# Retention and a two-layer MLP in split fp32: first products of two token blocks side by side in one 512-column matmul, in the second half of the weight units

## The chip, the cores and the metric

The kernel runs on one core of a Trainium2 chip. The metric is the device time of one execution in microseconds, the median of several. TensorE (PE in the profile) multiplies: a stationary operand of 128x128 is loaded (PEld), a moving operand of up to 512 columns streams against it, and the result goes to one of eight PSUM banks of 512 fp32 columns. ScalarE (ACT), VectorE (DVE) and GpSimd (POOL) do the elementwise work; SyncE (SP) issues nearly all DMAs.

## The reference

The first part is retention without softmax over 8 batches, 8 heads, 576 positions and 64 dimensions; its output, as 4608 tokens of 512, goes through a two-layer MLP of width 2048 with a PReLU whose slope depends on the channel.

```python
scores = scale * np.matmul(q, k.transpose(0, 1, 3, 2))
Dmat = np.where(rel >= 0, gamma[:, None, None] ** rel[None, :, :], 0.0)
x = np.matmul(scores * Dmat, v)                    # -> (4608, 512)
h = x @ w_in                                       # 512 -> 2048
g = np.maximum(h, 0.0) + alpha * np.minimum(h, 0.0)
out = g @ w_out                                    # 2048 -> 512
```

## The kernel before, in words

**Split products.** To keep fp32 precision at the faster rate of the fp32r type, each fp32 operand of the MLP is split into pieces (`split_x`, `split_g`, `split_w`), three planes that TensorE reads as fp32r. A product is then three matmuls in place of one: two go into one PSUM bank or half bank, the third into another, and an elementwise step joins the two.

**Tiling.** Tokens are cut into 18 blocks of 256 (`kb`). The hidden width is cut into eight *units* of 256 (`u`), each with four weight tiles: two for the first product, two for the second. Weights in three planes don't all fit, so the work is done in *visits*: visits 0 to 16 take blocks 0 to 16 with units 0 to 3 and keep the partial output in DRAM (`o_kept`); visit 17 takes block 17 with all eight units; visits 18 to 34 take blocks 0 to 16 again with units 4 to 7 and add the partial output (`evacuate`). A visit with one unit is a *cell*. The first eight cells are done in plain fp32 (`unit_plain`, L991, and `second_plain`, L1022), while weights are still converted.

**A cell.** `unit` makes the first product: for each half `f` of the unit, 12 matmuls of 256 columns (three planes, four parts of the 512 inputs) into bank `psh[f]`, whose two halves take the two sums (L1056). Then four operations on 256 columns: ScalarE copies one sum (L1063), VectorE joins (L1064), ScalarE takes the Relu of the negative into PSUM (L1067), VectorE applies the slope (L1070). `split_g` makes the three planes of g: two ScalarE multiplies (L1079, L1081) and two GpSimd subtractions (L1083, L1086). `second` makes the second product, 12 matmuls of 512 columns into the four banks `pso` (L1107), which gather over the units of a visit; the last cell of a visit is followed by `evacuate` (L1125, L1130) and a store. The second product of a cell comes `LAG` = 2 cells after its first.

**x.** `fetch_x` loads a block's x (or takes it from the retention stage), `split_x` makes its planes in one of two buffers `lxs`: ScalarE L957 and L961 or L969, VectorE L964, GpSimd L971 and L974. From visit `LATE_X` on the banks `psa` serve as scratch.

**Retention.** The first eight pairs of heads are done in a start-up phase (`part_...`, L447 to L595); the others one by one between the cells (`joint`, L808, L859 to L869), at the cells listed in `todo`. They use banks `psa` and `psh`.

**Order.** The text emits operations with estimated costs (`do`); `plan` then runs a list schedule over all of them: it works out due times from the end backwards and gives every engine its fixed order of instructions. TensorE may be taken up to `AHEAD_PE` operations ahead of the text. Engines run their own order and wait for each other by semaphores; `lock=True` marks operations of GpSimd and VectorE that are ordered against each other.

Of the kernel before, what the change touches and what calls it, by code (L numbers as in the profile page):

```python
# [16 lines left out]
ACTF = mybir.ActivationFunctionType  # L17
# [4 lines left out]
def kernel(  # L22
# [58 lines left out]
    def piece(x):  # L81
        return x.bitcast(PIECE)
# [108 lines left out]
    def do(eng, cost, fn, r=(), w=(), late=0.0, lock=False, kind=None, hold=0.0):  # L191
        deps, gens = set(), []
        for keys, writes in ((r, False), (w, True)):
            for g, *sub in keys:
                wr, rd = g.keys.setdefault(tuple(sub), ([], []))
                deps.update(wr)
                if writes:
                    deps.update(rd)
                deps.update(g.before)
                if g not in gens:  # L200
                    gens.append(g)
        op = Op(eng, cost, fn, None, [g.slot for g in gens if g.slot and g.slot.bank], late, lock, hold)
        for g, *sub in w:
            g.keys[tuple(sub)] = ([op], [])
        for g, *sub in r:
            g.keys[tuple(sub)][1].append(op)
        for g in gens:
            assert not g.slot or g.slot.gen is g
            g.ops.append(op)
        op.deps = [d for d in deps if d is not op]  # L210
        op.gens, op.kind = gens, kind or eng
        ops.append(op)
        return op
# [123 lines left out]
    AHEAD_PE = 150  # L337
    BACKLOG, HOLD = 2.0, 30.0
    LAG, HOLD_X = 2, 100.0
    GROUPS = (("v0",), ("v1",), ("x", "su"))  # L340
    SLACK, SWITCH = {"PE": 0.3}, {"PE": 0.1}
    BEGIN = {"PE": 5.0, "ACT": 0.5, "DVE": 8.2, "POOL": 5.8, "SP": 0.5}
# [395 lines left out]
    def w_piece(u, i, l):  # L738
        g, n = w_at[u, i][l]
        return piece(words_of(g)[:, n * DM:(n + 1) * DM])  # L740
# [207 lines left out]
                [(xkm[kb], 0)], [(x, 0)])  # L948
        vis["from"] = x

    def split_x(vis):
        x = vis["from"]
        to = vis["x"] = Gen(lxs[vis["n"] % 2])
        keys = [(x, *s) for s in x.keys]
        for n in range(2):
            c = slice(2 * n, 2 * n + 2)
            do("ACT", 0.64, lambda c=c: nc.scalar.mul(piece(to.get()[:, 0, c]), x.get()[:, c],  # L957
                                                      BELOW * 2.0 ** -12), keys, [(to, 0, n)])
            if vis["n"] >= LATE_X:
                h = Gen(psa[n])  # L960
                do("ACT", 0.6, lambda c=c, h=h: nc.scalar.mul(  # L961
                    piece(h.get()), x.get()[:, c].rearrange("p c t -> p (c t)"), BELOW), keys,
                    [(h, 0)])
                do("DVE", 0.7, lambda c=c, h=h: nc.vector.tensor_tensor(  # L964
                    out=piece(to.get()[:, 1, c].rearrange("p c t -> p (c t)")),
                    in0=x.get()[:, c].rearrange("p c t -> p (c t)"), in1=h.get(),
                    op=ALU.subtract), keys + [(h, 0)], [(to, 1, n)])
            else:
                do("ACT", 0.64, lambda c=c: nc.scalar.mul(piece(to.get()[:, 2, c]), x.get()[:, c],  # L969
                                                          BELOW), keys, [(to, 2, n)])  # L970
                do("POOL", 1.29, lambda c=c: nc.gpsimd.tensor_tensor(  # L971
                    out=piece(to.get()[:, 1, c]), in0=x.get()[:, c], in1=to.get()[:, 2, c],
                    op=ALU.subtract), keys + [(to, 2, n)], [(to, 1, n)], lock=True)
            do("POOL", 1.29, lambda c=c: nc.gpsimd.tensor_tensor(  # L974
                out=piece(to.get()[:, 2, c]), in0=to.get()[:, 0, c], in1=to.get()[:, 1, c],
                op=ALU.subtract), [(to, 0, n), (to, 1, n)], [(to, 2, n)], lock=True)


    def unit_plain(cell):
# [60 lines left out]

    def unit(cell):
        vis, u = cell["vis"], cell["u"]
        x = vis["x"]
        ga = Gen(gas[cell["n"] % 2])
        for f in range(2):
            ph = Gen(psh[f])

            def at(b, ph=ph):
                return ph.get()[:, b * TB:(b + 1) * TB]

            def mm(f=f, at=at):
                for n, (b, l) in enumerate(((0, 0), (1, 2), (0, 1))):
                    for cc in range(NCC):
                        w = w_piece(u, cc // 2, l)
                        c0 = (cc % 2 * 2 + f) * P
                        nc.tensor.matmul(at(b), w[:, c0:c0 + P],  # L1056
                                         piece(x.get()[:, l, cc]), start=(n == 0 and cc == 0),
                                         stop=(n > 0 and cc == NCC - 1), skip_group_check=True)
            do("PE", 1.43, mm, [(x, l, n) for l in range(3) for n in range(2)] +
               [w_at[u, i][l] for i in range(2) for l in range(3)], [(ph, 0), (ph, 1)], kind="pieces")  # L1060
            fc = 2 * u + f
            g = lambda f=f: ga.get()[:, f]
            do("ACT", 0.36, lambda g=g, at=at: nc.scalar.copy(g(), at(1)), [(ph, 1)], [(ga, f)])  # L1063
            do("DVE", 0.42, lambda g=g, at=at: nc.vector.scalar_tensor_tensor(  # L1064
                out=g(), in0=at(0), scalar=ONE, in1=g(), op0=ALU.mult, op1=ALU.subtract),
                [(ph, 0)], [(ga, f)])
            do("ACT", 0.39, lambda g=g, at=at: nc.scalar.activation(at(1), g(), ACTF.Relu,  # L1067
                                                                    scale=-1.0),
               [(ga, f)], [(ph, 1)])
            do("DVE", 0.48, lambda g=g, at=at, fc=fc: nc.vector.scalar_tensor_tensor(  # L1070
                out=g(), in0=at(1), scalar=malpha[:, fc:fc + 1], in1=g(), op0=ALU.mult,
                op1=ALU.add), [(ph, 1), (cst, "a")], [(ga, f)])
        cell["ga"] = ga

    def split_g(cell):
        ga = cell["ga"]
        to = cell["g"] = Gen(gs[cell["n"] % 3])
        both = [(ga, 0), (ga, 1)]
        do("ACT", 0.64, lambda: nc.scalar.mul(piece(to.get()[:, 2]), ga.get(), BELOW), both,  # L1079
           [(to, 2)])  # L1080
        do("ACT", 0.64, lambda: nc.scalar.mul(piece(to.get()[:, 0]), ga.get(), BELOW * 2.0 ** -12),  # L1081
           both, [(to, 0)])
        do("POOL", 1.29, lambda: nc.gpsimd.tensor_tensor(  # L1083
            out=piece(to.get()[:, 1]), in0=ga.get(), in1=to.get()[:, 2], op=ALU.subtract),
            both + [(to, 2)], [(to, 1)], lock=True)
        do("POOL", 1.29, lambda: nc.gpsimd.tensor_tensor(  # L1086
            out=piece(to.get()[:, 2]), in0=to.get()[:, 0], in1=to.get()[:, 1], op=ALU.subtract),
            [(to, 0), (to, 1)], [(to, 2)], lock=True)
# [168 lines left out]

    ready_kb = [((kb + 1) * TB - 1) // S for kb in range(NKB)]
    todo = {}
    for i, at in enumerate((8, 10, 12, 14, 16, 18, 20, 22, 25, 27, 29, 31, 33, 35, 37, 39, 41, 43, 45, 47, 49, 51, 53, 55)):  # L1260
        todo.setdefault(at, []).append(2 * NPAIR + 1 + i)
    assert sum(map(len, todo.values())) == len(pairs) - 2 * NPAIR

# [21 lines left out]
    def planes():  # L1285
        for x in (kxs, qxs, kns[0], kns[1], kTs[0], kTs[1], qTs[0], qTs[1]):
            yield Gen(x), 0
        for x in (ats, xs[4]):
            g = Gen(x)
            yield g, 0  # L1290
            yield g, 1

    def start_x(vis):
        kb = vis["kb"]
        if "from" not in vis and (kb not in xb or NPAIR * (ready_kb[kb] + 1) in done):
            fetch_x(vis)

    pend = []
    for cell in cells[8:]:
        n, vis = cell["n"], cell["vis"]  # L1300
        start_x(vis)
        if "x" not in vis:
            split_x(vis)
        for _ in range(ahead.get(n, 0)):
            convert((op_, 0), was, None)
        for at in late.get(n, ()):
            if at == 16:
                plane = planes()
            split_w(at, raw_room(), [next(plane) for _ in range(3)] if at < 20 else None)
        unit(cell)  # L1310
        pend.append(cell)
        if len(pend) > LAG:
            second(pend.pop(0))
        split_g(cell)
        for x in todo.get(n, ()):
            joint_(x)
        nxt = vis["n"] + 1
        if nxt < len(visits) and (cell["last"] or vis["n"] > 3):
            start_x(visits[nxt])
            if "from" in visits[nxt] and "x" not in visits[nxt] and cell["last"]:  # L1320
                split_x(visits[nxt])
    for cell in pend:
        second(cell)
    best = plan()

    port = None
# [39 lines left out]
```

## Time and profile before

| | |
|---|---|
| median of 3 runs | 949.26 us (947.74 to 952.68) |
| the profiled execution | 948.37 us, of which its span is 946.7 us |
| TensorE busy, granted clock | 924.4 us (98%), 1.00 |
| VectorE, ScalarE, GpSimd busy | 549.3, 572.0, 576.6 us |
| first products, 256 columns (L1056) | 2832 matmuls in the largest group, 284 ns each |
| second products, 512 columns (L1107) | 1416 matmuls in the largest group, 392 ns each |
| DMA | 121.06 MB, 128 GB/s |

The durations of matmuls overlap their neighbours, so that their sum says nothing of the pace; the distance between the starts of two does. Busy shares are averages over stages: the first 108 us are start-up, then retention and MLP alternate up to about 442 us, the rest is MLP alone.

### The profile page before, as it was taken

The page shows a single profiled execution, that of the slowest core. Times are in us where ns is not written, and L with a number is a line of the kernel's source. Part 1 is how long each engine was busy: PE and PEld are TensorE (multiplying, and loading weights), DVE is VectorE, ACT ScalarE, POOL GpSimd, SP SyncE. Part 2 cuts the span into 40 slices and gives each one's busy share as a digit, 9 for nine tenths or more (in the row PEclk, how much of TensorE's full clock was granted, in tenths as well). Part 3 has the DMA queues.
Part 4 walks back from the last instruction along what each step waited for, and adds up shares of the span by engine and source line. Part 5 has one row for each costly group of instructions (what it writes and reads, how often), then busy time and mean ns, then how long its engine had stood idle before and what let it go on. Part 6 is the DMA issues. An engine that isn't in the chain of part 4 may idle for free.

```text
span 946.7 us, 22947 instructions
## 1 busy us (share of the span) xinstructions
PE 924.4 (98%) x9009; PEld 817.5 (86%) x9009; DVE 549.3 (58%) x1180; ACT 572.0 (60%) x1285; POOL 576.6 (61%) x473
## 2 busy tenths in 40 slices
PE   5899999999999999999999999999999999999998
PEld 4566688988898899888999999999999999999997
DVE  6667566666677676677655844444445444444444
ACT  4465556557666566667867875555555555555443
POOL 3757766738767666746764475555555555555543
PEclk9999999999999999999999999999999999999999
DMA  9967587876878878874433511222222222122211
GB/s 225 226 182 132 142 186 164 183 166 164 204 177 183 199 166 200 192 179 147 145 123 123 179 36 50 83 86 83 67 68 68 68 67 68 68 67 68 67 46 68
DMA packets 235533, 121.06 MB, mean 128 GB/s; under 512 B 203408, under 2 KB 203424, under 8 KB 235424
## 3 DMA queue, kind: packets, MB, share of 16 engines
q1 hardware_dynamic: 233312, 119.05, 48.4%
q8 instruction: 71, 1.16, 0.5%
q10 hardware_dynamic: 2112, 0.53, 0.3%
q14 instruction: 38, 0.31, 0.1%
HBM read 74.19 MB, written 31.98 MB: 112 GB/s over the span
## 4 chain that ended last, share of the span: by engine, by line
PE 92%; DMA 3%; ACT 2%; SPq 1%; DVE 1%; issue 0%; POOL 0%; ACTq 0%; DVEq 0%
PE psh L1056 41%; PE pso L1107 39%; PE psh L808 3%; PE pso L1022 3%; PE psh L991 2%; PE psa L869 2%; SPq L220 1%; ACT x L571 1%; DMA w<-in_q_dram 1%; PE psh L859 1%; PE psa L866 1%; DMA lx<-in_moe_w_out_dram 0%; DMA w<-in_k_dram 0%; DMA lx<-in_moe_w_in_dram 0%; DMA w<-in_moe_w_in_dram 0%
## 5 line engine op out<-in xcount | busy, mean ns | idle before, releaser
L1056 PEld LDWEIGHTS psh<-lx,w 128*128 128x128 f32 x2832 | 355.9, 191 | 11.4 <-issue 0.5
L1056 PE MATMUL psh<-lx,w 128*128 128x256 f32 x2832 | 363.7, 284 | 0.1
L1107 PE MATMUL pso<-w,g 128*128 128x512 f32 x1416 | 347.8, 392 | 0.0
L1083 POOL TENSOR_TENSOR g<-ga,g 128x512 fp32r<-128x512 f32 x136 | 175.7, 1292 | 240.6 <-ACT g L1079 212.7
L1107 PEld LDWEIGHTS pso<-w,g 128*128 128x128 f32 x1416 | 257.1, 189 | 47.9
L1064 DVE SCALAR_TENSOR_TENSOR ga<-psh,ga 128x256 f32<-128x256 f32 x272 | 114.8, 422 | 212.6 <-ACT ga L1063 209.6
L1063 ACT COPY ga<-psh 128x256 f32<-128x256 f32 x272 | 101.4, 373 | 160.3 <-PE psh L1056 145.2
L1086 POOL TENSOR_TENSOR g<-g 128x512 fp32r<-128x512 f32 x136 | 176.0, 1294 | 16.2 <-DVE wa L690 2.8
L1070 DVE SCALAR_TENSOR_TENSOR ga<-psh,malpha,ga 128x256 f32<-128x256 f32 x272 | 130.3, 479 | 57.5 <-ACT psh L1067 55.8
L1067 ACT ACTIVATE psh<-ga 128x256 f32<-128x256 f32 x272 | 105.8, 389 | 71.0 <-DVE ga L1064 70.5
L1079 ACT ACTIVATE g<-ga 128x512 fp32r<-128x512 f32 x136 | 85.9, 632 | 55.2 <-DVE ga L1070 46.8
L974 POOL TENSOR_TENSOR lx<-lx 128x512 fp32r<-128x512 f32 x66 | 85.3, 1295 | 38.4 <-DVE lx L964 30.6
L1081 ACT ACTIVATE g<-ga 128x512 fp32r<-128x512 f32 x136 | 84.3, 620 | 0.0
L887 DVE SCALAR_TENSOR_TENSOR at<-psa,pf,mask 64x512 f32<-64x512 f32 x48 | 36.0, 750 | 21.4 <-PE psa L866 20.2
L957 ACT ACTIVATE lx<-x 128x512 fp32r<-128x512 f32 x66 | 41.1, 628 | 0.0
L808 PEld LDWEIGHTS psh<-at,vn 128*64 128x64 f32 x864 | 27.5, 138 | 8.9 <-issue 6.4
L780 POOL TENSOR_TENSOR qx<-qx,tabx 128x576 f32<-128x576 f32 x24 | 27.5, 1147 | 12.1 <-DVE wa L690 7.6
L971 POOL TENSOR_TENSOR lx<-x,lx 128x512 fp32r<-128x512 f32 x24 | 31.0, 1293 | 6.2 <-ACT lx L969 5.2
L808 PE MATMUL psh<-at,vn 128*64 128x64 f32 x864 | 31.4, 225 | 0.5 <-DVE ga L1070 0.5
L964 DVE TENSOR_TENSOR lx<-x,psa 128x512 fp32r<-128x512 f32 x42 | 28.4, 677 | 3.3 <-PE psh L1056 2.1
L1056 PE MATMUL psh<-lx,kT 128*128 128x256 f32 x144 | 29.0, 283 | 0.0
L869 PE MATMUL psa<-vn,kn 64*64 64x64 f32 x768 | 28.5, 223 | 0.0
(210 smaller groups left out, 1085.9 us busy)
## 6 DMA issues: line engine op xcount, KB each, us to landing
xk<-x SPq DMA_DIRECT2D x18, 512.0 KB, 4.3
out_dram<-o SPq DMA_DIRECT2D x36, 256.0 KB, 2.0
ok<-o SPq DMA_DIRECT2D x34, 256.0 KB, 3.4
x<-xk SPq DMA_DIRECT2D x17, 512.0 KB, 5.0
op<-ok SPq DMA_DIRECT2D x17, 512.0 KB, 3.9
qx<-in_q_dram SPq DMA_DIRECT2D x96, 72.0 KB, 2.9
kx<-in_k_dram SPq DMA_DIRECT2D x96, 72.0 KB, 2.7
kn<-in_k_dram SPq DMA_DIRECT2D x48, 144.0 KB, 3.3
```

The lines of the kernel that those rows point to most:

```text
L808: nc.tensor.matmul(pv[i].get()[half(h2), (j - js[0]) * C:(j - js[0] + 1) * C], vns[n % 2][:, h2, j], mt.get()[:, h2, j], start=True, stop= ...
L974: do("POOL", 1.29, lambda c=c: nc.gpsimd.tensor_tensor(out=piece(to.get()[:, 2, c]), in0=to.get()[:, 0, c], in1=to.get()[:, 1, c], op=ALU. ...
L1056: nc.tensor.matmul(at(b), w[:, c0:c0 + P], piece(x.get()[:, l, cc]), start=(n == 0 and cc == 0), stop=(n > 0 and cc == NCC - 1), skip_grou ...
L1063: do("ACT", 0.36, lambda g=g, at=at: nc.scalar.copy(g(), at(1)), [(ph, 1)], [(ga, f)])
L1064: do("DVE", 0.42, lambda g=g, at=at: nc.vector.scalar_tensor_tensor(out=g(), in0=at(0), scalar=ONE, in1=g(), op0=ALU.mult, op1=ALU.subtrac ...
L1067: do("ACT", 0.39, lambda g=g, at=at: nc.scalar.activation(at(1), g(), ACTF.Relu, scale=-1.0), [(ga, f)], [(ph, 1)])
L1070: do("DVE", 0.48, lambda g=g, at=at, fc=fc: nc.vector.scalar_tensor_tensor(out=g(), in0=at(1), scalar=malpha[:, fc:fc + 1], in1=g(), op0=A ...
L1079: do("ACT", 0.64, lambda: nc.scalar.mul(piece(to.get()[:, 2]), ga.get(), BELOW), both, [(to, 2)])
L1081: do("ACT", 0.64, lambda: nc.scalar.mul(piece(to.get()[:, 0]), ga.get(), BELOW * 2.0 ** -12), both, [(to, 0)])
L1083: do("POOL", 1.29, lambda: nc.gpsimd.tensor_tensor(out=piece(to.get()[:, 1]), in0=ga.get(), in1=to.get()[:, 2], op=ALU.subtract), both + [ ...
L1086: do("POOL", 1.29, lambda: nc.gpsimd.tensor_tensor(out=piece(to.get()[:, 2]), in0=to.get()[:, 0], in1=to.get()[:, 1], op=ALU.subtract), [( ...
L1107: nc.tensor.matmul(a[2 * m + b].get(), piece(g.get()[:, l, f, m * P:(m + 1) * P]), w_piece(u, 2 + f, l), start=(cell["first"] and f == 0 a ...
```

## The change

After visit 17, visits are taken in pairs: 18 with 19, up to 32 with 33; visit 34 is left alone. For a pair the planes of x of both blocks are laid side by side (`two_rooms`): in the two `lxs` buffers for odd pairs, in the four weight slots of unit 3, which is no longer needed, for even ones. A first product (`unit_two`) then takes 512 columns, both blocks at once, into two whole banks: `psh` for the first half of a unit, `psa` for the second. The four elementwise operations work on 512 columns. Their result goes to one of five rooms (`ga_room`: three x buffers and the two buffers of v that retention has left), since a cell of the second block waits until the first block's four cells are done. The second products stay as they are for each cell, but are drawn from a queue (`pump`), so many after each half unit as `PUMP` says; `split_g` is done for the two cells at the queue's head. `split_x` makes its pieces in SBUF alone, with a VectorE subtraction, where it fills such a pair. Some planes of late weights move to other buffers (`planes`), and the cells at which the pairs of heads begin are respaced (`todo`).

The diff, cut to its core:

```diff
+    PUMP0, PUMP = ((1, 1), (0, 1), (0, 1), (0, 1)), ((1, 2), (1, 2), (0, 1), (0, 1))
...
+    def two_rooms(n):
+        if n % 2:
+            gg = [Gen(x) for x in lxs]
+            return {(l, cc): (gg[cc // 2], (l * 2 + cc % 2) * DM)
+                    for l in range(3) for cc in range(NCC)}, DM
+        gg = [Gen(wsl[NS - 1, i]) for i in range(4)]
+        at = {(2, cc): (gg[cc], 2 * DM) for cc in range(NCC)}
+        at.update({(l, cc): (gg[l * 2 + cc // 2], cc % 2 * DM)
+                   for l in range(2) for cc in range(NCC)})
+        return at, DM
...
+                    eng, cost, tt = (("POOL", 1.29, nc.gpsimd) if rooms is None else
+                                     ("DVE", 0.69 if wide else 0.42, nc.vector))
+                    do(eng, cost, lambda c=c, l=l, d=d, tt=tt: tt.tensor_tensor(
+                        out=piece(l()), in0=raw(c), in1=d(), op=ALU.subtract),
+                        keys + key(2, c), key(1, c), lock=True)
...
+    def unit_two(va, vb, u, ga, f):
+        at_x = va["x"][0]
+        p0, p1 = (Gen(x) for x in (psa if f else psh))
+
+        def mm():
+            for p, l in ((p0, 0), (p1, 2), (p0, 1)):
+                for cc in range(NCC):
+                    w = w_piece(u, cc // 2, l)
+                    c0 = (cc % 2 * 2 + f) * P
+                    g, o = at_x[l, cc]
+                    nc.tensor.matmul(p.get(), w[:, c0:c0 + P], piece(words_of(g)[:, o:o + DM]),
+                                     start=(l != 1 and cc == 0), stop=(l > 0 and cc == NCC - 1))
+        do("PE", 2.755, mm, x_keys(va, 0) + x_keys(vb, 1) +
+           [w_at[u, i][l] for i in range(2) for l in range(3)], [(p0, 0), (p1, 0)], kind="pieces")
+        fc = 2 * u + f
+        g = lambda: words_of(ga)[:, f * DM:(f + 1) * DM]
+        do("ACT", 0.59, lambda: nc.scalar.copy(g(), p1.get()), [(p1, 0)], [(ga, f)])
+        do("DVE", 0.69, lambda: nc.vector.scalar_tensor_tensor(
+            out=g(), in0=p0.get(), scalar=ONE, in1=g(), op0=ALU.mult, op1=ALU.subtract),
+            [(p0, 0)], [(ga, f)])
+        do("ACT", 0.62, lambda: nc.scalar.activation(p1.get(), g(), ACTF.Relu, scale=-1.0),
+           [(ga, f)], [(p1, 0)])
+        do("DVE", 0.75, lambda: nc.vector.scalar_tensor_tensor(
+            out=g(), in0=p1.get(), scalar=malpha[:, fc:fc + 1], in1=g(), op0=ALU.mult,
+            op1=ALU.add), [(p1, 0), (cst, "a")], [(ga, f)])
...
-        to = cell["g"] = Gen(gs[cell["n"] % 3])
+        to = cell["g"] = Gen(gs[ng[0] % 3])
+        ng[0] += 1
...
-    for i, at in enumerate((8, 10, 12, 14, 16, 18, 20, 22, 25, 27, 29, 31, 33, 35, 37, 39, 41, 43, 45, 47, 49, 51, 53, 55)):
+    for i, at in enumerate((8, 10, 12, 14, 16, 18, 20, 22, 24, 26, 29, 31, 33, 35, 37, 39, 42, 44, 46, 48, 50, 52, 54, 56)):
...
+    queue = list(pend)
+
+    def ahead_g(k=2):
+        for c in queue[:k]:
+            if "ga" in c and "g" not in c:
+                split_g(c)
+
+    def pump(k):
+        for _ in range(k):
+            if queue and "ga" in queue[0]:
+                ahead_g(1)
+                second(queue.pop(0))
+                ahead_g()
+
+    for i, (va, vb) in enumerate(two):
+        ca, cb = of[va["n"]], of[vb["n"]]
+        queue += ca + cb
+        for nu, (a, b) in enumerate(zip(ca, cb)):
+            ga = ga_room()
+            for f in range(2):
+                unit_two(va, vb, a["u"], ga, f)
...
+                    ahead_g()
+                pump((PUMP if i else PUMP0)[nu][f])
+            nxt = va["n"] + 2 + (nu - 1)
+            if nu in (1, 2) and nxt < len(visits):
+                next_x(visits[nxt])
```

## The prediction

> **What bounds the kernel now.** I read the page first: engine shares, the forty slices, the chain, the costliest groups.
>
> ```profile
> PE 924.4 (98%) x9009; PEld 817.5 (86%) x9009; DVE 549.3 (58%) x1180; ACT 572.0 (60%) x1285; POOL 576.6 (61%) x473
> ...
> PE   5899999999999999999999999999999999999998
> PEld 4566688988898899888999999999999999999997
> ...
> PEclk9999999999999999999999999999999999999999
> ...
> PE 92%; DMA 3%; ACT 2%; SPq 1%; DVE 1%; issue 0%; POOL 0%; ACTq 0%; DVEq 0%
> ```
>
> TensorE is busy in every slice but the first two, at full granted clock, and carries 92% of the chain that ended last. No other engine passes 61%. A change therefore pays only if it shortens TensorE's own work, and costs only if it makes TensorE wait. The list of TensorE's waits shows that nearly all of them lie in the start-up:
>
> ```profile
> PE psa L447 <- DMA w<-in_k_dram: 4.3, 1, 4.3
> PE psh L991 <- ACT x L571: 3.3, 2, 2.0
> PE pso L447 <- POOL w L423: 3.3, 2, 2.9
> ...
> PE psh L808 <- DVE ga L1070: 0.5, 1, 0.5
> ```
>
> L447 and L991 are start-up code; L808 is the only entry of the stage after it. The stretch that is changed begins near 450 us. Its table of windows and its timeline of TensorE:
>
> ```profile
> 600.00:900.00 300.00, 300.00 (x1928) 274.00 (x1928) 140.68 (x291) 167.89 (x372) 173.41 (x136) 1.00 0.21 69
> ```
>
> ```profile
> 700.88 3.04 PE L1056 MATMUL psh<-lx,w 128*128 128x256 f32 x24
> 703.75 0.63 PE L1107 MATMUL pso<-qT,g 128*128 128x512 f32 x2
> ...
> 706.50 3.04 PE L1056 MATMUL psh<-lx,w 128*128 128x256 f32 x24
> 709.37 2.91 PE L1107 MATMUL pso<-w,g 128*128 128x512 f32 x12
> ```
>
> The columns of the first are TensorE, weight load, VectorE, ScalarE, GpSimd: TensorE is never idle in 300 us, VectorE is busy 47%, ScalarE 56%, GpSimd 58%. In the second the start times give the true pitch, because durations overlap: 24 first-product matmuls of 256 columns take 703.75 - 700.88 = 2.87 us (119.6 ns each), 12 second-product matmuls of 512 columns 706.50 - 703.75 = 2.75 us (229.2 ns each). A cell costs 5.62 us and nothing waits.
>
> **The change, part by part.**
>
> *First products side by side.* The visits 18 to 33 make eight pairs; each has four weight units and two halves of a unit, so 64 calls of `unit_two` with 12 matmuls of 512 columns. They replace 128 half units of 12 matmuls of 256 columns, 1536 instructions by 768. The shape (128x128 weights, 512 moving columns, the same piece type) is that of the second product, so I take its 2.75 us for twelve. Two cells then cost 2 x 2.75 = 5.50 us in place of 2 x 2.87 = 5.74 us: 0.24 us for each of 32 pairs of cells, **7.7 us** (0.01 us of reading error on each start makes this 7 to 8.5).
>
> A rule speaks against that. The Trainium skill, "TensorE: Matmul & The Clock Gate", section "Back-to-back issue gap", gives the gap of an isolated matmul as its columns over 2.4 GHz and about 2.5 ns more. Joining two matmuls would then save 2.5 ns, and 768 joins 1.9 us: too little to see. The rows above have 2 x 119.6 - 229.2 = 10 ns. The rows are of this stream, with its own weight loads, so I keep 10 ns; the rule gives the low end of the gain.
>
> *Evacuating them.* Each call is followed by a copy, a subtraction, a Relu and a multiply-add on 512 columns in place of two sets on 256. Nearest rows: ScalarE copies from PSUM 128x512 0.59 us (L1129), writes to PSUM 0.59 (L961), VectorE 0.69 (L1130): 0.59 + 0.69 + 0.59 + 0.69 = 2.56 us and some 0.04 us at each hand-over. Before it was 0.37 + 0.42 + 0.39 + 0.48 = 1.66. Work falls: four operations of 2.56 us replace eight of 3.3 us. The chain is 0.9 us longer; what covers it is the distance in the built order of TensorE. Four banks now serve the first products, psh for one half and psa for the other, two at a time. In the tightest place two halves are followed by half a second product and two more halves, so a bank is wanted 2.75 + 1.37 = 4.1 us after its matmuls end, and the second bank of the two 0.9 us later still. The copy can start 0.9 us before the end, since the bank it reads is finished after eight of the twelve. About 2.2 us are needed, 4.1 to 5.0 there are: cost nothing. Without the cover, a call would wait for the missing part.
>
> *Splitting g.* Unchanged per cell: two ScalarE multiplies (0.63 + 0.62) and two GpSimd subtractions (1.29 + 1.29). In the trace a cell's last copy starts at 602.79 and its g is complete at 606.67 + 1.30 = 607.97: 5.2 us, so about 6.1 us with the longer chain. In the built order the shortest distance to the second product that reads it is two second products and one half unit, 2 x 2.75 + 2.75 = 8.2 us. Covered, by 2 us. Here is the new wait: with cells queued (A0 to A3, then B0 to B3) the ScalarE multiply of a cell waits for one of three g buffers, which the second product three places earlier frees. Behind it in ScalarE's queue stand the copy and the Relu of the next half, on which VectorE and then a PSUM bank depend.
>
> *Splitting x.* The psa banks are no longer scratch. A visit's x is split with ScalarE (four operations, or six in the visits whose planes lie in the freed weight slots), VectorE (two of 0.68 us, or four shorter) and GpSimd (two of 1.30, or four shorter), reading SBUF only. The VectorE subtraction now has both operands in SBUF and is ordered against GpSimd's. Per pair of visits, 16 x 2.75 = 44 us of TensorE, GpSimd has 8 x 2.58 + 4 x 1.30 = 25.8 us, ScalarE 8 x 1.18 + 8 x 1.25 + 5 = 24.4, VectorE 8 x 1.38 + 5.5 + 2.7 = 19.2. Each is under 60%: no new bound. DMA counts hardly change; the two x loads of a pair are issued together on SP some 20 us ahead of their ScalarE reader, against 5.0 us to landing in the DMA rows; SP's stores of earlier outputs stand in front of them and are done by then.
>
> *The turn.* The first pair's x can be split only when weight unit 3 has had its last second product. From there to the first 512-column matmul the order has two 256-column first products and three second products, 2 x 2.87 + 3 x 2.75 = 14.0 us. In it GpSimd must do two cells' g and eight quarter subtractions, 2 x 2.58 + 8 x 0.7 = 10.8 us, in turns with VectorE's eight of about 0.42 (L1064 has that size), 3.4 us: 14.2 us. That is tight. Bounds 0 to 3 us; I take **+1.0**, nearer the low end because the last-needed planes are read 0.9 us into the first call.
>
> *Visit boundaries.* Before, a first product (2.87 us) stood between the last second product of a visit and the first of the next. Now at eight places they abut. The bank wanted first is free once the first half's two VectorE operations (0.68 + 0.69) end, and the other half's 1.37 us of matmuls covers one of them, since the other can start early; a 0.69 us operation of the x or g work in front makes it late. Bounds 0 to 0.7 us each, 5.6 in all; I take **+0.5** in all.
>
> *Begins of the pairs respaced.* Work is the same. TensorE has 0.5 us of idle named between 110 and 450 us, so there is nothing to win but a little in the start-up, where the order of a few blocks shifts (TensorE is busy 90.1 of the first 107.6 us). Bounds -1.5 to +1.5; I take 0. The tail has the same sequence as before, a half second product and then three, 42 matmuls after the last first product: 0.
>
> Sum on the profiled execution: 948.37 - 7.7 + 1.0 + 0.5 = 942.2 us (its span is 946.7, 1.7 lies around it). That execution lies 0.9 us under the median of 949.26 and inside the runs shown, so I forecast **942.4 us**, nearly on its basis.
>
> **Rivals.** What a measurement of this kernel can tell from no change is about 0.5%, 4.7 us: faster means under 944.5, slower over 954.0.
>
> 1. *The gain is real and hidden waits take half of it, or the pitch is nearer the rule.* For: the turn and the abutting boundaries have 0 to 8.6 us of room for loss, and with 2.5 ns a join the gain is 1.9. Against: every cover worked out above is over 1 us except at the turn. Upper half of the bounds: 948.4 - 7.7 + 3 + 2.5 = 946.2; with the rule's pitch 948.4 - 1.9 + 0.5 = 947.0. Time **946.5**.
>
> 2. *Slower: ScalarE's queue stops on g buffers.* In the build order up to six split multiplies of three cells stand in a row, two of them waiting for a second product to free their buffer. If the head waits, the next half's copy waits behind it, its bank comes free late, TensorE stops, and so does the second product that should free the buffer sooner. Place: each of the 64 calls; it decides from 12.4 us in all, 0.2 us a call, on top of the 2 to 3 us of cover. At 0.4 us a call: 948.4 - 7.7 + 25.6 = **966**. Against: ScalarE is busy 24.4 of 44 us and the distances are 8 us.
>
> That the change does not do what it says is excluded: the built order holds the 512-column first products and 1536 fewer 256-column ones.
>
> **How the numbers follow.** The forecast has 0.80, rival 1 0.14, rival 2 0.06. The first's own range is 939.5 to 944.5 (start-up 1.5 better and pitch 8.5 at one end, the turn at 3 us at the other). To hold 8 in 10 with room for rival 1: 939.5 to 946.8. Faster by over 0.5% 0.79, within 0.5% 0.15, slower 0.06.
>
> **What would show it.** Right: the new first-product line has 12 starts in 2.75 us; TensorE's windows from 500 us on are full; the g buffers and psa appear in no TensorE wait; the last second product ends about 6 us earlier. Turn wrong: a TensorE gap near 440 to 446 us released by GpSimd or VectorE. Boundaries: gaps of a few tenths before second products, released by VectorE. Rival 2: gaps before the new line released by VectorE, with ScalarE waiting on TensorE. The forecast is wrong if the 512-column first product keeps a pitch over 235 ns, or if idle TensorE after 450 us passes 4 us.

## The result, and the profile after

The changed kernel takes a median of **941.69 us** (940.02 to 942.44, five runs) against 949.26 us (947.74 to 952.68) for the kernel before: a ratio of 0.9908, 95% interval 0.9882 to 0.9933. The forecast was 942.4 us. The profiled execution of the kernel after took 940.2 us, with a span of 938.5 us.

From the page of the kernel after, first the busy times, then three rows of the forty slices and the chain that ended last:

```profile
PE 915.6 (98%) x8241; PEld 777.7 (83%) x8241; DVE 532.7 (57%) x1070; ACT 552.9 (59%) x1175; POOL 578.2 (62%) x491
...
PE   5898999999999999999999999999999999999998
PEld 4666688888889898888899988888888888888887
...
PEclk9999999999999999999999999999999999999999
...
PE 89%; POOL 3%; issue 2%; DVE 1%; ACT 0%; POOLq 0%; ACTq 0%; DVEq 0%
```

TensorE has 768 matmuls and 8.8 us of busy time less, and its 98% share is what it was: the bound has not moved, it has become shorter. VectorE and ScalarE fell as well, by 16.6 and 19.1 us, mainly because four operations on 512 columns replace eight on 256. In the chain, 3% of GpSimd and 2% of issue are new. The two lines of GpSimd with most of it belong to the start-up: L424 scales inputs of the retention, L733 splits weights, and the last of these ends at 116 us.

The list of TensorE's waits in the kernel after (line that waited, what released it; total us, how often, the longest):

```profile
PE psa L448 <- DMA w<-in_k_dram: 4.0, 1, 4.0
PE pso L448 <- POOL w L424: 3.8, 2, 3.3
PE psh L1039 <- POOL lx L694: 1.8, 2, 1.6
...
PE psh L809 <- DVE ga L1122: 0.9, 2, 0.6
PE psh L860 <- ACT x L828: 0.9, 1, 0.9
```

L448 and L1039 are start-up, as before. L809 and L860 belong to the retention stage between 107 and 450 us. From 450 us on, where the change works, there is no entry at all: neither a g buffer nor a psa bank ever stops TensorE. The window of 600 to 900 us says the same; TensorE's own column is full, with nearly a third fewer matmuls in it (1327 for 1928):

```profile
600.00:900.00 300.00, 300.00 (x1327) 247.57 (x1327) 127.37 (x200) 151.22 (x276) 172.88 (x148) 1.00 0.20 68
```

In the timeline of TensorE the difference of two starts is the true time of a group:

```profile
604.12 2.88 PE L1189 MATMUL pso<-w,g 128*128 128x512 f32 x12
606.84 2.88 PE L1138 MATMUL psh<-lx,w 128*128 128x512 f32 x12
609.56 2.88 PE L1189 MATMUL pso<-w,g 128*128 128x512 f32 x12
612.28 2.88 PE L1138 MATMUL psa<-lx,w 128*128 128x512 f32 x12
615.00 2.88 PE L1189 MATMUL pso<-w,g 128*128 128x512 f32 x12
```

Twelve first-product matmuls of 512 columns take 609.56 - 606.84 = 2.72 us (226.7 ns each), and so do the twelve second-product matmuls beside them, which had taken 2.75 us in the kernel before.

### The profile page after: what moved, and what is told of

Same layout as the page of the kernel before. It is cut to its first block, busy times and chain, and to the rows that moved or that the text cites. A ratio compares the mean times of both kernels' runs of the same rounds, so it can differ in the third digit from the quotient of the medians.

```text
span 938.5 us, 21278 instructions
## 1 busy us (share of the span) xinstructions
PE 915.6 (98%) x8241; PEld 777.7 (83%) x8241; DVE 532.7 (57%) x1070; ACT 552.9 (59%) x1175; POOL 578.2 (62%) x491
## 4 chain that ended last, share of the span: by engine, by line
PE 89%; POOL 3%; issue 2%; DVE 1%; ACT 0%; POOLq 0%; ACTq 0%; DVEq 0%
PE pso L1189 40%; PE psh L1108 22%; PE psh L1138 9%; PE psa L1138 9%; PE psh L809 3%; PE psa L870 2%; PE pso L1070 1%; POOL w L424 1%; PE psh L1039 1%; POOL w L733 1%; PE psa L867 1%; PE psh L860 1%; DVE w L735 1%; POOL lx L694 0%; POOL g L694 0%
## 5 line engine op out<-in xcount | busy, mean ns | idle before, releaser
L1189 PE MATMUL pso<-w,g 128*128 128x512 f32 x1416 | 345.1, 391 | 0.0
L1189 PEld LDWEIGHTS pso<-w,g 128*128 128x128 f32 x1416 | 260.1, 188 | 51.0 <-POOL g L1168 0.4
L1108 PE MATMUL psh<-lx,w 128*128 128x256 f32 x1608 | 209.1, 285 | 0.1
L1108 PEld LDWEIGHTS psh<-lx,w 128*128 128x128 f32 x1608 | 202.1, 191 | 7.5 <-issue 0.8
L1168 POOL TENSOR_TENSOR g<-g 128x512 fp32r<-128x512 f32 x136 | 175.8, 1293 | 20.9 <-DVE lx L1014 3.4
L1165 POOL TENSOR_TENSOR g<-ga,g 128x512 fp32r<-128x512 f32 x72 | 93.0, 1292 | 125.7 <-ACT g L1161 94.0
L1116 DVE SCALAR_TENSOR_TENSOR ga<-psh,ga 128x256 f32<-128x256 f32 x144 | 60.6, 421 | 62.6 <-ACT ga L1115 60.4
L1115 ACT COPY ga<-psh 128x256 f32<-128x256 f32 x144 | 53.6, 372 | 70.2 <-PE psh L1108 63.1
L1165 POOL TENSOR_TENSOR g<-x,g 128x512 fp32r<-128x512 f32 x40 | 51.7, 1292 | 62.0 <-ACT g L1161 59.7
L1122 DVE SCALAR_TENSOR_TENSOR ga<-psh,malpha,ga 128x256 f32<-128x256 f32 x144 | 68.6, 477 | 22.5 <-ACT psh L1119 21.8
L1018 POOL TENSOR_TENSOR lx<-lx 128x512 fp32r<-128x512 f32 x48 | 61.8, 1294 | 23.0 <-DVE lx L1014 12.9
L1119 ACT ACTIVATE psh<-ga 128x256 f32<-128x256 f32 x144 | 55.7, 387 | 26.9 <-DVE ga L1116 26.3
L1161 ACT ACTIVATE g<-ga 128x512 fp32r<-128x512 f32 x72 | 45.5, 632 | 24.2 <-DVE ga L1122 14.8
L1163 ACT ACTIVATE g<-ga 128x512 fp32r<-128x512 f32 x72 | 44.7, 620 | 0.0
L1145 DVE SCALAR_TENSOR_TENSOR x<-psh,x 128x512 f32<-128x512 f32 x20 | 13.8, 689 | 43.9 <-PE psh L1138 42.9
L809 PEld LDWEIGHTS psh<-at,vn 128*64 128x64 f32 x864 | 27.5, 138 | 10.6 <-issue 6.8
L1138 PE MATMUL psh<-lx,w 128*128 128x512 f32 x144 | 34.7, 390 | 0.0
```

What stands on the lines that cost most here:

```text
L809: nc.tensor.matmul(pv[i].get()[half(h2), (j - js[0]) * C:(j - js[0] + 1) * C], vns[n % 2][:, h2, j], mt.get()[:, h2, j], start=True, stop= ...
L1018: lambda l=l, d=d, h=view(0, c): nc.gpsimd.tensor_tensor(out=piece(d()), in0=h(), in1=l(), op=ALU.subtract),
L1108: nc.tensor.matmul(at(b), w[:, c0:c0 + P], xp(l, cc), start=(n == 0 and cc == 0), stop=(n > 0 and cc == NCC - 1), skip_group_check=True)
L1138: nc.tensor.matmul(p.get(), w[:, c0:c0 + P], piece(words_of(g)[:, o:o + DM]), start=(l != 1 and cc == 0), stop=(l > 0 and cc == NCC - 1))
L1165: do("POOL", 1.29, lambda: nc.gpsimd.tensor_tensor(out=piece(to.get()[:, 1]), in0=whole(), in1=to.get()[:, 2], op=ALU.subtract), both + [( ...
L1168: do("POOL", 1.29, lambda: nc.gpsimd.tensor_tensor(out=piece(to.get()[:, 2]), in0=to.get()[:, 0], in1=to.get()[:, 1], op=ALU.subtract), [( ...
```

## The experiments

### The width alone: split256

The changed kernel, with each 512-column matmul of the first product issued as two of 256. Its trace has every engine's operations in the same order as the kernel after:

```diff
-                    nc.tensor.matmul(p.get(), w[:, c0:c0 + P], piece(words_of(g)[:, o:o + DM]),
-                                     start=(l != 1 and cc == 0), stop=(l > 0 and cc == NCC - 1))
+                    for s0 in (0, TB):
+                        nc.tensor.matmul(p.get()[:, s0:s0 + TB], w[:, c0:c0 + P],
+                                         piece(words_of(g)[:, o + s0:o + s0 + TB]),
...
```

> The changed kernel with the same order on every engine, the same banks, buffers and evacuation, but each 512-column first product issued as two of 256 columns, one for each block. Width theory (a fixed cost per matmul, about 13 ns on TensorE, is all of the gain): 768 joins undone at 2 x 119.4 - 226.7 = 12.1 ns are 9.3 us, and the second products next to a 256-column product go back from 2.72 to 2.75 us, up to 1.5 us more: 951 to 953 us, the new line at 2.87 us for 24. Order theory (the gain comes from the queue of second products, the longer covers and the respaced pairs): stays at 941 to 943.

Measured: 951.0 us (949.77 to 953.96), ratio to before 1.0011 [1.0, 1.0021]. The gain is gone. From the timeline of TensorE in split256:

```profile
606.68 2.88 PE L1192 MATMUL pso<-w,g 128*128 128x512 f32 x12
609.40 3.04 PE L1139 MATMUL psh<-lx,w 128*128 128x256 f32 x24
612.27 2.91 PE L1192 MATMUL pso<-w,g 128*128 128x512 f32 x12
615.02 3.04 PE L1139 MATMUL psa<-lx,w 128*128 128x256 f32 x24
617.89 2.91 PE L1192 MATMUL pso<-w,g 128*128 128x512 f32 x12
```

The first product is back at 612.27 - 609.40 = 2.87 us, and the second product after it takes 615.02 - 612.27 = 2.75. Over the whole stage, from the first start of a paired first product to the start of the last second product, split256 takes 946.15 - 561.43 = 384.72 us and the kernel after 934.42 - 560.54 = 373.88: a difference of **10.84 us**. Added up from the starts, 9.71 us of it lie in the first products (183.98 against 174.27) and 1.12 us in the second products next to them (189.24 against 188.12). So the width explains all of the gain, and somewhat more than it: everything else that the change does costs about 1 us (0 to 2 by the interval above), or 2.7 us by the two profiled spans (10.84 less the 8.2 us from 946.7 to 938.5).

The first of these is touched by the granted clock, of which the kernel before had more low values here. Of its runs beside this experiment and the later ones, the 18 with a mean clock of 1.000 average 948.3 us and the 17 at 0.993 or 0.994 average 952.3. Like with like, on the chip of split256: its three runs at 1.000 average 950.6 us, the nine of the kernel before at 1.000 average 948.3. That puts the rest of the change at about 2.3 us of loss.

### Narrower still: split128

The same loop with four matmuls of 128 columns:

```diff
-                    nc.tensor.matmul(p.get(), w[:, c0:c0 + P], piece(words_of(g)[:, o:o + DM]),
+                    for s0 in range(0, DM, P):
+                        nc.tensor.matmul(p.get()[:, s0:s0 + P], w[:, c0:c0 + P],
+                                         piece(words_of(g)[:, o + s0:o + s0 + P]),
...
```

> As split256, with each 512-column first product issued as four of 128 columns. It asks what the cost per matmul is. Fixed cost per matmul (theory): the pitches 226.7 (512 columns) and 119.4 ns (256) lie on a line of 0.419 ns a column and 12.1 ns, so 128 columns take 65.7 ns, 4 x 65.7 - 226.7 = 36 ns more for each of 768: 941.7 + 27.8 = 969 to 972 us. Weight load as the bound below 256 columns (rival: the 119 ns of 256 columns are already the pace of loading 128x128 weights): 128 columns also take about 119 ns, 4 x 119 - 226.7 = 249 ns more: 941.7 + 191 = 1133 us.

Measured: 1114.04 us, ratio 1.1733 [1.1702, 1.1765]. From its timelines, first of TensorE's matmuls, then of its weight loads:

```profile
701.24 2.88 PE L1192 MATMUL pso<-w,g 128*128 128x512 f32 x12
703.96 5.47 PE L1139 MATMUL psh<-w,w 128*128 128x128 f32 x48
709.27 2.99 PE L1192 MATMUL pso<-w,g 128*128 128x512 f32 x12
```

```profile
703.74 5.55 PEld L1139 LDWEIGHTS psh<-w,w 128*128 128x128 f32 x48
```

48 matmuls take 709.27 - 703.96 = 5.31 us, 110.6 ns each; over all 3072 of them it is 340.61 us, 110.9 ns. The straight line through the other two widths (119.6 ns at 256, 226.7 at 512) gives 66 ns at 128, so the idea of columns plus one fixed cost is false below 256. There is one weight load for each matmul, also for the four that use the same weights, and their lane is busy from end to end (5.55 us for 48, no gap): a pace of about 111 ns for a weight load fits. But the lane has no gap at 256 columns either (split256):

```profile
609.17 3.05 PEld L1139 LDWEIGHTS psh<-lx,w 128*128 128x128 f32 x24
```

So the full lane does not single out the load. That a narrow matmul streams more slowly in itself would give the same time, and no run separates the two: the cause of the 111 ns stays open. The expectation that put the load's pace at that of the 256-column matmul was 19 us too long.

### The respacing alone: only_begins and old_begins

The kernel before with the new `todo`, and the kernel after with the old one:

```diff
-    for i, at in enumerate((8, 10, 12, 14, 16, 18, 20, 22, 25, 27, 29, 31, 33, 35, 37, 39, 41, 43, 45, 47, 49, 51, 53, 55)):
+    for i, at in enumerate((8, 10, 12, 14, 16, 18, 20, 22, 24, 26, 29, 31, 33, 35, 37, 39, 42, 44, 46, 48, 50, 52, 54, 56)):
```

> The kernel before with nothing but the new begins. Width theory: no gain, 948 to 951 us, at worst 1.5 us slower by the same wait of the last pair. Respacing theory: 942 to 946.

Measured: 948.25 us, ratio 0.9991 [0.998, 1.0002]. On the kernel before, the respacing is worth nothing that can be told.

> The changed kernel with the begins of the pairs of heads as they were before. Width theory: the gain stays, 940 to 942.5 us; it may win 0.9 to 1.5 us, since the trace of the changed kernel has a TensorE wait of 0.9 us at L860 before the last pair and loses 1.5 us more than the kernel before between 433 and 458 us. Respacing theory (the new begins carry the gain or were needed for it): 945 or more.

Measured: 942.51 us, ratio 0.9916 [0.99, 0.9932], 0.8 us above the kernel after, which the intervals do not separate. With the start-up left out, from the first score matmul (L860) to the end of the span, it takes 833.3 us against 831.7. Its waits of TensorE from 107 to 945 us show what the respacing is there for:

```profile
PE pso L1189 <- DVE o L1212: 2.2, 1, 2.2
PE pso L1189 <- ACT o L1211: 1.2, 1, 1.2
PE psh L809 <- DVE ga L1122: 0.9, 2, 0.6
```

With the old begins, two second products between 360 and 420 us wait for the evacuation of the visit before, 3.4 us in all; with the new ones these two are gone and 0.9 us at L860 appears. The respacing repairs a small fault that the new order would have had, by the single traces about 1.6 us.

### The g buffers: two_g_buffers

Two g buffers in place of three from the turn on, to bring on the wait of the prediction's slow rival:

```diff
-        to = cell["g"] = Gen(gs[ng[0] % 3])
+        to = cell["g"] = Gen(gs[ng[0] % (2 if cell["vis"]["n"] > turned_to else 3)])
```

> The changed kernel with two g buffers in place of three from visit 18 on; the order of TensorE stays the same up to the lone last visit. It takes away the cover that the second rival of the prediction doubted. If the cover is wide: a g buffer is freed at least 5.4 us of TensorE before it is read again, against 3.4 us for the split, so only GpSimd's x operations in between (1.3 to 3 us) can make it late: 0 to 6 us slower, 942 to 948. If ScalarE's wait for the buffer is what TensorE lives close to: over 10 us slower, above 952, with TensorE waits at the second product released by GpSimd.

Measured: 941.71 us, ratio 0.9913 [0.9887, 0.9939]: no change from the kernel after. ScalarE's waits from 600 to 900 us, of the kernel after:

```profile
ACT g L1161 <- PE pso L1189: 26.0, 28, 1.6
```

and of two_g_buffers, in the same window:

```profile
ACT g L1161 <- PE pso L1189: 47.8, 39, 2.2
```

The wait exists, and nearly doubles with a buffer fewer. TensorE does not notice: its list of waits is that of the kernel after. What the prediction feared is real on ScalarE and has no way to the end time.

### The banks: two_banks

Both halves of a unit in the `psh` banks, `psa` unused. The scheduler knows of the banks and arranges the order anew, so the order is not that of the kernel after:

```diff
-        p0, p1 = (Gen(x) for x in (psa if f else psh))
+        p0, p1 = (Gen(x) for x in psh)
```

> The changed kernel with banks psh alone for both halves of a unit; psa is not used by the first products. It takes away the cover of the longer evacuation chain: where two halves follow each other, the next one's second bank is free 2.1 us after the end of the last, and is wanted 0.9 us after it, so 1.2 us of TensorE are lost there. In the built order 25 to 30 such places are left, since the scheduler puts second products between the others: 30 to 36 us slower at most, 960 to 978 us, with TensorE waits at the first products released by VectorE. If the banks were no cover that matters: 941 to 944.

Measured: 993.42 us, ratio 1.0466 [1.0447, 1.0484], 51.7 us above the kernel after. TensorE's waits from 107 us on:

```profile
PE pso L1189 <- POOL g L1168: 12.1, 19, 0.9
PE psh L1138 <- DVE x L1145: 10.2, 12, 0.9
PE psh L1138 <- DVE vn L1145: 4.3, 5, 0.9
PE psh L1138 <- DVE x L1150: 2.7, 12, 0.2
PE pso L1189 <- DVE o L1212: 1.9, 4, 0.6
```

In 17 of the 64 halves TensorE now waits twice for VectorE to empty a bank: about 0.9 us before the first matmul (L1145, 12 and 5 in two rows), and 0.2 us before the fifth, which needs the second bank (L1150). The delay goes on into g and the second product (L1168). It cost more than expected because of this second link: of the loss, 29.8 us lie in the first products and 20.8 us in the second. The four-operation evacuation is hidden only by the alternation of the two pairs of banks, which is the part of the change that lets the wide matmul pay.

### Begins between old and new: begins_24, begins_mixed, mixed_cost

If old and new begins each have a small wait in one place, a mixture may have neither. begins_24 takes the old list up to the sixteenth begin and the new one after it; begins_mixed takes the new list, but 41, 43, 45 in place of 42, 44, 46:

```diff
-24, 26, 29, 31, 33, 35, 37, 39, 42, 44, 46, 48, 50, 52, 54, 56
+25, 27, 29, 31, 33, 35, 37, 39, 42, 44, 46, 48, 50, 52, 54, 56   # begins_24
+24, 26, 29, 31, 33, 35, 37, 39, 41, 43, 45, 48, 50, 52, 54, 56   # begins_mixed
```

> The changed kernel with its later begins from the 17th on (42 to 56), and the early ones of before (25, 27). Two effects were seen: the new late begins cost a TensorE wait of 0.9 us at L860 and some switches, the old ones let TensorE wait 3.4 us for an evacuation before the first pair of visits. If both hang on the late begins, this is the changed kernel again: 941 to 942.5. If the early begins matter, up to 1.5 us either way.

> The changed kernel with the old begins 41, 43, 45 in the middle and the new ones from 48 on. Width theory: the gain stays whatever the begins are, 940.5 to 943; a better spread can only win back part of the 2.5 us that the changed kernel loses before its first 512-column product.

begins_24: 941.46 us, ratio 0.9915 [0.9896, 0.9933], the same as the kernel after. begins_mixed: 938.75 us, ratio 0.9888 [0.9873, 0.9902]. Its waits of TensorE from 107 us on are a single line:

```profile
PE psh L809 <- DVE ga L1122: 0.9, 2, 0.6
```

The L860 wait is gone and the L1189 waits have not come back. (begins_24 has a wait of 0.5 us at L1189 in place of the one at L860.) To see whether the remaining 3 us are real, the kernel after and begins_mixed ran again on another chip, with a third version that also gives the scheduler the measured duration (`do("PE", 2.72, ...)` for 2.755 in `unit_two`):

> The changed kernel as it is, on one chip with the two below, so that they can be compared without a change of chip in between: 940 to 942.5 us.

> The kernel begins_mixed once more. If its lead is of the order of the begins (its trace lacks the 0.9 us wait at L860 that the changed kernel has): 1 to 2 us under after_again, in every round. If its 938.75 was the chip or the start-up: equal within 0.5 us.

> begins_mixed with the measured 2.72 us as the scheduler's cost of twelve 512-column first products in place of 2.755. The order before the first of them stays, later a half second product less stands between two halves. Nothing waits there, so the same as mixed_again within 0.5 us; a bank wait of VectorE would show as 1 us or more.

| | median us | ratio to before, same chip | first score matmul to end of span, us |
|---|---|---|---|
| after_again | 941.42 (939.72 to 942.78) | 0.9909 [0.989, 0.9929] | 831.6 |
| mixed_again | 940.42 (939.64 to 946.57) | 0.9912 [0.9886, 0.9937] | 830.7 |
| mixed_cost | 939.14 (938.27 to 944.97) | 0.9901 [0.9873, 0.9928] | 830.3 |

The intervals overlap. The last column leaves the start-up out; there the mixture gains 0.9 us both times (830.8 in its first run, 831.7 in the kernel after), which is the L860 wait, and the new cost figure 0.3 more. That much is plausible and the medians do not prove it. The lead of 3 us in the first run of begins_mixed did not come back (1.0 us the second time).

Much of that goes with the granted clock. Three of the four first runs of begins_mixed had a mean clock of 1.000, and none of the five of the kernel after was above 0.998; other versions at 1.000 were as quick (begins_24 938.55 and 939.73 us, mixed_cost 938.31 and 939.29). In the profiled runs, up to the last matmul, the clock is below 1.00 in the start-up only, in stretches of about 3.4 us in which it is 0.50. The first 107 us of old_begins, which has none, and of begins_24, which has 10.2 us at 0.50:

```profile
0.00:107.00 107.00, 88.94 (x1639) 64.81 (x1643) 70.98 (x152) 54.90 (x99) 65.30 (x72) 1.00 0.79 187
```

```profile
0.00:107.00 107.00, 88.86 (x1589) 64.32 (x1590) 69.69 (x150) 53.54 (x98) 63.48 (x70) 0.95 0.78 187
```

The third column from the end is the clock, 1.00 and 0.95. The first score matmul starts at 106.4 us in old_begins, at 108.2 in after_again (0.97), at 109.7 in begins_24. A start-up that moves by this much can hide or feign a gain of 3 us.

## Why the prediction was right

- **The bound** was read rightly: TensorE alone, full in every slice, so that only its own pace counts. VectorE and ScalarE lost 16.6 and 19.1 us of work beside it, which bought nothing by themselves.
- **The pitch** was right in its mechanism and small in its size: 7.7 us forecast, 10.84 measured with the order held fixed. The term took the 512-column first product at the 2.75 us of L1107, which stood next to 256-column groups; with 512 on both sides both kinds take 2.72. The 0.03 us come off the first product and off its neighbour, and the latter was not in the sum at all.
- **The rule against it** did not carry over to this stream. The Trainium skill, "TensorE: Matmul & The Clock Gate", section "Back-to-back issue gap", states columns over 2.4 GHz and 2.5 ns for an isolated matmul; an estimate from it gave 1.9 us for 768 joins. Measured, the excess over the columns at that rate is 119.6 - 106.7 = 12.9 ns at 256 and 226.7 - 213.3 = 13.4 ns at 512, and the joins saved 9.71 us in the first products themselves. Taking the pitch from this stream's own rows, as the prediction did, was the choice that mattered.
- **The turn** was forecast at +1.0 us and cost nothing. It was also misplaced: it lies at 560 us, not at 440 to 446, about the length of the start-up (108 us) later; how 440 was counted is not on record. TensorE's timeline at the first 512-column matmul, then GpSimd's (in square brackets the idle time before the operation and what ended it):

```profile
554.80 5.90 PE L1189 MATMUL pso<-w,g 128*128 128x512 f32 x24
560.54 0.61 PE L1138 MATMUL psh<-w,kx 128*128 128x512 f32 x2
```

```profile
551.23 4.23 POOL L1018 TENSOR_TENSOR w<-w,w 128x256 fp32r<-128x256 f32 x6 [0.54 <-DVE w L1014]
555.42 1.30 POOL L1165 TENSOR_TENSOR g<-ga,g 128x512 fp32r<-128x512 f32 x1
556.80 1.29 POOL L1168 TENSOR_TENSOR g<-g 128x512 fp32r<-128x512 f32 x1
558.96 1.44 POOL L1018 TENSOR_TENSOR w<-w,w 128x256 fp32r<-128x256 f32 x2 [0.87 <-DVE w L1014]
```

  The eighth quarter subtraction ends at 558.96 + 1.44 = 560.40 us, 0.14 us before the matmul at 560.54 starts. By the order of planes in `unit_two`, what it writes is read by the second four of the twelve matmuls, so that there was another 0.9 us or more to spare. "That is tight" was right; the loss it was given did not occur.
- **The boundaries**, +0.5 us forecast, cost nothing: no wait of TensorE is listed between 450 and 940 us.
- **Evacuation, g, x, loads** were costed at nothing because of stated covers, and cost nothing. two_banks shows that the first cover was doing work (51.7 us without the second pair of banks), two_g_buffers that the second was wide (22 us more of ScalarE's waiting from 600 to 900 us, none of TensorE's).
- **The order ahead of the pairs** was forecast at 0 within -1.5 to +1.5, and is where the rest of the gain went: 1 us by split256's ratio, 2.7 by the spans, 2.3 at a like clock, so most likely outside the stated bounds. 1.3 us of it are listed waits, L860 and L809 with 1.8 us against L808 with 0.5 before; for the rest the runs do not tell order from spread, and its cause stays open. The errors have opposite signs (3.1 us of gain too little and 1.5 us of waits too many, against up to 2.7 us of order too few). That the total came within 0.7 us of the median, closer than its terms, is in part luck.
- **The rivals.** Half the gain, or the rule's pitch: refuted by split256 and the empty list of waits. The queue on g buffers: refuted by two_g_buffers, even with a buffer fewer.

## What to carry to other kernels

When TensorE is full and everything else has slack, fewer and wider matmuls are worth what the distance between starts says they are in this same stream, so take the pitch of both widths from the timeline, and from groups whose neighbours are as they will be. The wide matmul is the easy part; what makes it pay is room for what follows it, here a second pair of PSUM banks and rooms for results that must wait. An order that is moved has to be looked at once more where nothing was meant to change: here about two microseconds went there.

## What the runs showed that was not expected

- A 128-column matmul with its own weight load is hardly faster than one of 256 columns: 110.9 ns against 119.6. Splitting the first product's 512 columns into four costs 172 us (medians); into two, 10.8 (over the paired stage).
- Groups of twelve 512-column matmuls take 2.72 us between others of 512 columns and up to 2.75 after a group of 256.
- The start-up of almost the same program ended at times from 105.7 to 111.1 us in single profiled runs of the versions of the kernel after. A lower granted clock goes with the late ends: it was 1.00 over the first 107 us in two_banks (105.7) and old_begins (106.4), 0.95 to 0.97 in begins_24 (109.7), after_again (108.2) and split128 (111.1). Differences of a microsecond are better read from the first start after the start-up than from the whole span.
